# A late-weight schedule in a fused attention and mixture-of-experts kernel: logits in three parts, one more resident piece, buffers laid out by when they die

## The chip, the cores and the metric

The kernel runs on one core of one Trainium2 chip. The metric is device time in microseconds (us), the median of the runs shown. TensorE (PE) does matrix products and transposes, VectorE (DVE) and ScalarE (ACT) work on vectors and read the matrix results from PSUM, GpSimd (POOL) works on vectors in SBUF and issues DMAs, and SyncE (SP) issues DMAs.

## The reference

Attention with one extra zero logit in the denominator, and on its output a soft mixture of eight experts (32 slots, four per expert). Cut to what matters:

```python
# q, k, v: (8, 12, 448, 64)
scores = q @ k.T / sqrt(64);  m = scores.max(-1);  e = exp(scores - m)
attn_out = (e / (e.sum(-1) + exp(-m) + 1e-9)) @ v
x = attn_out as (3584, 768)                     # 12 heads side by side

logits = x @ phi                                # (3584, 32)
d = softmax of logits over the 3584 tokens      # one column per slot
slot_input = d.T @ x                            # (32, 768)
for e in range(8):                              # four slots per expert
    slot_out[e] = relu(slot_input[e] @ w1[e]) @ w2[e]    # 768 -> 1024 -> 768
c = softmax of logits over the 32 slots
out = c @ slot_out                              # (3584, 768)
```

The logits of a token need all twelve heads of its batch entry. The softmax over tokens needs all batch entries, so the experts can run only after the last attention tile.

## The kernel before

**Pairs and steps.** A unit u (0 to 23) is a pair of batch entries and a pair of heads; six units in a row make one group of two batch entries, and there are four such groups. Attention runs in steps n; unit u begins at step 7u. Step n computes one score tile (stage_S, line 200, whose row maximum DVE takes at line 208) and, ten steps behind (LAG), one transposed score tile (stage_ST: lines 236 and 241, with the exponential on ACT at line 245). The maximum reaches stage_ST as a mask md, which stage_MT (lines 214 to 226, on ACT and POOL) makes at step 7u+7. stage_AV (line 271) multiplies the exponentials by the values at steps 7u+13 to 7u+18; stage_AVout, stage_den and stage_N (lines 281 to 299) normalise, and stage_X (lines 345 and 347) transposes the result x to xt.

**An order written out by hand.** Nothing is reordered: a dictionary `plan` maps a step and a place in it ("small", then the step's stage_S, "value", stage_ST, "end", "load") to functions, and every engine and every DMA queue takes its instructions in that order. An engine does not keep step with the others: it runs ahead until an instruction has to wait, and everything behind that instruction waits too. POOL's instruction queue holds its vector work, the q and k loads and all weight loads (line 129). SP's holds the value loads (line 98).

**Values.** load_v fills `vr`, of which there is one; stage_V (line 250) casts it to bf16 into v65 or v66 and sets a column of ones (line 252). Both are planned at step 7u+9, the cast first and then the load for the next unit.

**Buffers.** All attention buffers are slices of one SBUF tile `block`, laid out by the dictionary `parts`. PSUM is a ring of three buffers (`slot`), handed out in program order, beside one for the value product (`av`).

**Mixture.** For each group of six units, mixture() plans, from step n = 42 bp + 62 on, the logits (line 379: 24 matmuls, four for each of the six head pairs, into one PSUM buffer, which ACT copies to lT at lines 386 and 387), the running maximum and exponential over tokens, slot_in (line 429, which reads the x of all six units) and the softmax over slots. In the last group five head pairs are summed at step n - 2 and the sixth at step n. There the experts follow: experts_hidden (line 553) with w1, and after the loop the product with w2 (line 642), the spread over partitions (line 651) and the output tiles (lines 665 to 670).

**Weights.** w1 and w2 come as 32 pieces of 768 KB: 16 of w1 first, then 16 of w2. The first WRES pieces have a place of their own in `wres` and are loaded during attention, one in nearly every unit. The others go into `rooms`, stretches of `block` over dead attention buffers:

```python
for n, i in ((end - 4, 0), (end + 3, 1), (end + 10, 2), (end + 12, 3), (end + 12, 4),
             (end + 12, 5), (end + 20, 6), (end + 27, 7), (end + 27, 8)):
    at(n, "load", lambda i=i: load_w(WRES + i))        # end = 168
```

The functions that the change touches:

Of the kernel before, what the change touches and what calls it, by code (L numbers as in the profile page):

```python
# [13 lines left out]
ALU = mybir.AluOpType  # L14
# [2 lines left out]
P = 64  # L17
LAG = 10
AV0 = (13, 14, 14, 15, 16, 17, 18)
WRES = 23  # L20


@with_exitstack
def kernel(
# [10 lines left out]
    nc = tc.nc  # L35

    B, H, S, D = q.shape
    DD = H * D
# [4 lines left out]
    TB = S // P  # L43
    KC = DD // 128
    FK = F // 128
    HP = H // 2
    BP = B // 2
    U = BP * HP
    C3 = TB // 2
    N2 = 2 * S  # L50
    G = E // 4
# [11 lines left out]

    HW = (KC // 2) * F
    parts, size = {}, 0
    for name, n, bufs in (("qr", N2, 1), ("kr", N2, 1), ("qk0", 2 * N2, 1), ("qk1", 2 * N2, 1),
                          ("vr", 2 * N2, 1), ("md0", N2, 1), ("v65", 2 * TB * 66, 1),
                          ("qk2", 2 * N2, 1), ("md1", N2, 1), ("v66", 2 * TB * 66, 1),
                          ("et", N2, 4), ("xu", 4 * TB * 65, 1),
                          ("x", N2, HP + 1), ("xt", N2, HP)):  # L70
        parts[name] = size, n, bufs
        size += n * bufs


    rooms = [i * HW for i in range(6)]
    rooms += [size - G * DD - HW, size - G * DD - 3 * HW, size - G * DD - 2 * HW]
    assert rooms[5] + HW <= parts["x"][0] + N2 <= rooms[7] and rooms[6] >= parts["xt"][0]
    block = const.tile([128, size], BF16, name="block")
    wres = const.tile([128, WRES, HW], BF16, name="wres")

    def buf(name, i):
        o, n, bufs = parts[name]
        return block[:, ds(o + (i % bufs) * n, n)]

    def room(i):

# [2 lines left out]
    def slot(shape, dtype=F32):  # L89
        return ring.tile(shape, dtype, tag="r", name="ps")  # L90
# [17 lines left out]
    def load_v(u):  # L108
        t_ = buf("vr", 0).bitcast(F32).rearrange("p (h n) -> p h n", h=2)
        RAW[u, "vr"] = load(u, t_, v, nc.sync if u else nc.gpsimd)  # L110
# [137 lines left out]
    def stage_V(u):  # L248
        t_ = buf(f"v6{5 + u % 2}", 0).rearrange("p (h t e) -> p h t e", h=2, e=66)
        nc.gpsimd.tensor_copy(t_[:, :, :, ds(0, D)],  # L250
                              RAW.pop((u, "vr")).rearrange("p h (t d) -> p h t d", t=TB))
        nc.gpsimd.memset(t_[:, :, :, ds(D, 1)], 1.0)
        V65[u] = t_
# [40 lines left out]
    def stage_N(u):  # L294
        xv = XU.pop(u)
        rec = small.tile([128, 2, TB], F32, tag="rec", name="rec", bufs=1)
        nc.vector.reciprocal(rec, DEN.pop(u))  # L297
        x = buf("x", u + 4).rearrange("p (s n) -> p s n", s=TB)
        nc.gpsimd.tensor_tensor(  # L299
            x.rearrange("p s (h d) -> p h s d", h=2), xv[:, :, :, ds(0, D)],  # L300
            rec.unsqueeze(3).broadcast_to([128, 2, TB, D]), op=ALU.mult)
        X[u] = x
# [12 lines left out]
    def stage_last(u):  # L315
        av = AV.pop(u)
        ems = DEN.pop(u)
        drec = small.tile([128, 2, TB], F32, tag="rec", name="rec", bufs=1).rearrange("p b g -> p (b g)")
        x = buf("x", u + 4).rearrange("p (s n) -> p s n", s=TB)
        main = av[:, :, ds(0, 2 * C3 * 65)].rearrange("p b (g e) -> p b g e", e=65)  # L320
        rest = av[:, :, ds(2 * C3 * 65, 65)]
        nc.vector.scalar_tensor_tensor(
# [35 lines left out]
    last_state = {}  # L358

    def mixture(bp, n, at):  # L360
# [9 lines left out]
        mx = small.tile([128, 8], F32, tag="mx", name="mx")  # L370
        sm = small.tile([128, 8], F32, tag="sm", name="sm")

        def logits_part(js):
            if js[0] == 0:
                last_state["lg"] = slot([128, 2, 128])
            ps = last_state["lg"]
            for j in js:
                for i, x in enumerate(groups(XT.pop(bp * HP + j))):
                    nc.tensor.matmul(ps[ds(32 * i, 32), ds(0, x.shape[1]), :], phi[:, j, :], x,
                                     start=(j == 0), stop=(j == KC - 1),  # L380
                                     tile_position=(0, 32 * i))

        def logits(js=range(KC)):
            logits_part(js)
            ps = last_state.pop("lg")
            nc.scalar.copy(lT[:, 0, :], ps[:, 0, :])
            nc.scalar.copy(lT[ds(0, 96), 1, :], ps[ds(0, 96), 1, :])

        def slot_max():
            if first:  # L390
# [80 lines left out]
            nc.scalar.copy(cT[ds(96, 32), bp, ds(0, 128)], ps[ds(96, 32), 0, :])  # L471

        if final:
            at(n - 2, "end", lambda: logits_part(range(KC - 1)))
            at(n, "end", lambda: logits((KC - 1,)))
            at(n + 2, "small", slot_max)
            at(n + 2, "end", gate_logits)
            at(n + 3, "small", slot_exp)
# [8 lines left out]
            at(n + 11, "small", gate_out)  # L487
            last_state["gate_T"] = gate_T
        else:
            at(n, "end", logits)  # L490
            at(n + 2, "end", slot_max)
            at(n + 3, "small", gate_logits)
            at(n + 5, "end", slot_exp)
# [67 lines left out]
    def at(n, where, f):  # L561
        plan.setdefault((n, where), []).append(f)

    for u in range(U):
        n = u * TB
# [2 lines left out]
        if u + 2 < U:  # L568
            at(n + 3, "load", lambda u=u: load_qk(u + 2))
        at(n + 7, "value", lambda u=u: stage_MT(u))  # L570
        at(n + 9, "load", lambda u=u: stage_V(u))
        if u + 1 < U:
            at(n + 9, "load", lambda u=u: load_v(u + 1))
        for m in sorted(set(AV0)):
            at(n + m, "value", lambda u=u, m=m: [
                stage_AV(u, [t for t in range(TB) if AV0[t] == m], part) for part in range(2)])
# [11 lines left out]
    for bp in range(BP):  # L588
        mixture(bp, (bp * HP + HP - 1) * TB + 27, at)

    for i, u in enumerate(sorted((*range(2, U - 1), 9, 16))):
        at(u * TB + 5, "load", lambda i=i: load_w(i))
    at(4, "load", late_constants)
    stage_T(0, "qr")
    stage_T(0, "kr")

    end = TB * U
    for n, i in ((end - 4, 0), (end + 3, 1), (end + 10, 2), (end + 12, 3), (end + 12, 4),
                 (end + 12, 5), (end + 20, 6), (end + 27, 7), (end + 27, 8)):
        at(n, "load", lambda i=i: load_w(WRES + i))  # L600
    last = max(n for n, _ in plan)

# [98 lines left out]
```

## Time and profile before

| | us |
|---|---|
| median of 3 runs | 343.98 |
| all runs | 346.65, 343.98, 342.94 |
| profiled execution, whole time | 345.78 |
| its span in the trace | 344.0 |

| engine | busy us | share of the span |
|---|---|---|
| PE | 289.1 | 84% |
| DVE | 255.8 | 74% |
| ACT | 207.5 | 60% |
| POOL | 202.8 | 59% |

The trace begins a little after the execution does and ends a little before it, so the span is shorter than the whole time. A row of a timeline gives start, duration, engine, line, operation, result and operands, count, and in brackets how long the engine had stood and what ended that. A row of the windows gives the busy time of each engine in a stretch (PE, weight loads, DVE, ACT, POOL, with instruction counts), the granted PE clock as a share of full speed, the busy share of the DMA engines and GB/s.

### The profile page before, as it was taken

The numbers are of one execution on the slowest core, as the hardware profiler recorded it, in microseconds if no ns is written. First come the engines' busy times: TensorE is split into PE (matmuls) and PEld (weight loads), VectorE is DVE, ScalarE is ACT, GpSimd is POOL, SyncE is SP. The second block draws the span as 40 slices with busy tenths as digits, with TensorE's granted clock in tenths as the row PEclk, the third lists the DMA queues.
The fourth block names the chain that finished last, engine by engine and source line by source line (L and its number), as shares of the span: only waits on it lengthen the run. The fifth ranks groups of instructions, "written<-read, shape, count | busy, mean of one in ns | idle before, by whom it ended". The sixth has DMA issues, their size and how long they took to land.

```text
span 344.0 us, 13196 instructions
## 1 busy us (share of the span) xinstructions
PE 289.1 (84%) x5864; PEld 161.7 (47%) x5864; DVE 255.8 (74%) x352; ACT 207.5 (60%) x327; POOL 202.8 (59%) x317
## 2 busy tenths in 40 slices
PE   2689999999999999987989979899989856858770
PEld 1335555555555565554655545465555433422110
DVE  2999898999889899988789979789877156016440
ACT  3037787777686677866677758676778840104340
POOL 8356676788767877767767866577636842200000
PEclk9999999999999999999999999999999985895555
DMA  6664799878898979988596999887864599945997
GB/s 87 115 99 93 138 195 168 166 160 156 169 196 143 210 147 197 194 155 160 106 193 129 215 200 150 149 155 147 163 147 84 108 182 216 214 84 207 396 399 281
DMA packets 30056, 59.09 MB, mean 172 GB/s; under 512 B 4048, under 2 KB 22224, under 8 KB 30000
## 3 DMA queue, kind: packets, MB, share of 16 engines
q0 software_dynamic: 19344, 36.69, 61.6%
q1 hardware_dynamic: 10656, 21.57, 19.0%
q8 instruction: 46, 0.75, 0.9%
q14 instruction: 10, 0.08, 0.1%
HBM read 83.46 MB, written 11.01 MB: 275 GB/s over the span
## 4 chain that ended last, share of the span: by engine, by line
PE 58%; ACT 14%; DMA 11%; DVE 8%; issue 5%; POOL 1%; SPq 0%; ACTq 0%; DVEq 0%; POOLq 0%
PE av L271 16%; PE ps L200 11%; PE ps L236 11%; PE ps L241 8%; ACT block L245 7%; PE ps L188 7%; DMA block<-in_moe_w_dram 6%; DVE m L208 5%; DMA out_dram<-wres 4%; ACT block L281 4%; ACT block L284 2%; PE ps L665 1%; DMA wres<-in_k_dram 1%; PE ps L429 1%; PE ps L212 1%
## 5 line engine op out<-in xcount | busy, mean ns | idle before, releaser
L208 DVE TENSOR_REDUCE m<-ps 128x2 bf16<-128x896 f32 x168 | 181.7, 1095 | 25.0 <-PE ps L200 21.9
L245 ACT ACTIVATE block<-ps 128x896 bf16<-128x896 f32 x168 | 154.0, 918 | 64.5 <-PE ps L241 58.5
L271 PE MATMUL av<-block 64*128 64x65 bf16 (+1 forms) x2688 | 82.8, 193 | 6.3 <-ACT block L284 2.3
L271 PEld LDWEIGHTS <-block 64*128 64x128 bf16 (+1 forms) x2688 | 70.0, 97 | 33.4 <-ACT block L284 9.5
L236 PE MATMUL ps<-block,ones 64*64 64x448 bf16 x672 | 69.1, 368 | 2.3 <-ACT block L245 0.9
L241 PE MATMUL ps<-block 64*64 64x448 bf16 x672 | 66.2, 352 | 1.9 <-issue 1.9
L220 POOL TENSOR_TENSOR block<-mt,nmask 128x768 bf16<-128x768 bf16 x24 | 35.2, 1466 | 45.9 <-ACT mt L214 43.6
L200 PE MATMUL ps<-block 64*128 64x448 bf16 x288 | 54.0, 372 | 3.3 <-DVE m L208 0.9
L200 PEld LDWEIGHTS <-block 64*128 64x128 bf16 x288 | 18.2, 94 | 55.2 <-issue 54.6
L299 POOL TENSOR_TENSOR block<-block,rec 128x896 bf16<-128x896 f32 x23 | 38.7, 1681 | 1.5 <-DVE rec L297 1.5
L98 POOL DMA_DIRECT2D block<-in_q_dram x46 | 29.4, 643 | 7.1 <-PE ps L188 6.8
L191 DVE COPY block<-ps 128x896 bf16<-128x896 bf16 x48 | 27.8, 616 | 4.4 <-PE ps L188 4.4
L236 PEld LDWEIGHTS <-ones 64*64 64x64 bf16 x672 | 25.6, 105 | 10.0 <-issue 2.9
L98 POOL DMA_DIRECT2D block<-in_k_dram x46 | 27.9, 626 | 2.3 <-issue 2.3
L188 PE MATMUL ps<-ident,block 128*64 128x128 bf16 x644 | 26.3, 229 | 3.2 <-issue 2.3
L188 PEld LDWEIGHTS <-block 128*64 128x64 bf16 x644 | 21.8, 114 | 5.7 <-issue 4.7
L241 PEld LDWEIGHTS <-block 64*64 64x64 bf16 x672 | 23.6, 107 | 0.4 <-issue 0.3
L665 PE MATMUL ps<-wres,cT 32*128 32x384 bf16 x56 | 19.1, 500 | 4.9 <-DVE wres L668 3.5
L250 POOL CAST block<-block 128x896 bf16<-128x896 f32 x24 | 22.3, 927 | 1.0 <-DMA block<-in_v_dram 1.0
L668 DVE COPY wres<-ps 128x768 f32<-128x768 f32 x14 | 13.4, 958 | 11.7 <-PE ps L665 8.4
L347 DVE COPY block<-ps 128x896 bf16<-128x896 bf16 x24 | 14.8, 616 | 9.6 <-PE ps L345 9.6
L668 ACT COPY wres<-ps 128x768 f32<-128x768 f32 x14 | 11.1, 799 | 14.7 <-DMA out_dram<-wres 9.8
(112 smaller groups left out, 241.3 us busy)
## 6 DMA issues: line engine op xcount, KB each, us to landing
wres<-in_moe_w_dram POOLq DMA_DIRECT2D x23, 768.0 KB, 9.0
out_dram<-wres SPq DMA_DIRECT2D x28, 384.0 KB, 4.7
block<-in_v_dram SPq DMA_DIRECT2D x46, 224.0 KB, 5.1
block<-in_moe_w_dram POOLq DMA_DIRECT2D x9, 768.0 KB, 13.6
block<-in_q_dram POOLq DMA_DIRECT2D x46, 112.0 KB, 4.4
block<-in_k_dram POOLq DMA_DIRECT2D x46, 112.0 KB, 5.4
block<-in_v_dram POOLq DMA_DIRECT2D x2, 224.0 KB, 4.4
wres<-in_q_dram POOLq DMA_DIRECT2D x2, 112.0 KB, 3.3
```

Of the source, the lines that this page charges most:

```text
L98: eng.dma_start(out=t_[ds(b * P, P), :, :], in_=src[bp * 2 + b, ds(hp * 2, 2)].rearrange("h (p t) d -> p h (t d)", t=TB))
L188: nc.tensor.transpose(ps[ds(h * D, D), :, ds(t * P, P)], r[:, h, ds(t * D, D)], ident)
L191: nc.vector.tensor_copy(t_, ps)
L200: nc.tensor.matmul(ps[:, h, ds(0, S)], QT[u][hs, b, ds(c * 128, 128)], KT[u][hs, b, :], start=True, stop=True)
L208: nc.vector.tensor_reduce(m[:, :, s], ps[:, :, ds(0, S)], axis=AX.X, op=ALU.max)
L220: nc.gpsimd.tensor_tensor(md[:, :, ds(0, C3 * 128)].rearrange("p b (c n) -> p b c n", c=C3), mt.unsqueeze(1).unsqueeze(1).broadcast_to([12 ...
L236: nc.tensor.matmul(ps[ds(b * P, P), h, ds(0, S)], ones[hs, :], MD[u][hs, b, :], start=True, stop=False)
L241: nc.tensor.matmul(ps[ds(b * P, P), h, ds(0, S)], KT[u][hs, b, ds(t * P, P)], QT[u][hs, b, :], start=False, stop=True)
L245: nc.scalar.activation(et, ps[:, :, ds(0, S)], AF.Exp, scale=scale)
L271: nc.tensor.matmul(o, et[bs, h, ds(c * 128, w)], V65[u][bs, h, t, ds(0, 65)], start=(t == 0 and h == 0 and c == 0), stop=(t == TB - 1), sk ...
L299: nc.gpsimd.tensor_tensor(x.rearrange("p s (h d) -> p h s d", h=2), xv[:, :, :, ds(0, D)], rec.unsqueeze(3).broadcast_to([128, 2, TB, D]), ...
L668: (nc.vector.tensor_copy if i % 2 else nc.scalar.copy)(o.rearrange("p (g n) -> p g n", g=2), ps[:, :, ds(0, 384)])
```

## The change

- **Logits in parts.** The six head pairs are summed as three pairs of two, at steps n - 28, n - 14 and n, each into a PSUM buffer of its own. The first part is copied to lT by ACT; the others are copied by ACT into lc and added to lT by POOL. In the last group the third part is summed as one head pair at n - 2 and one at n, and DVE adds it to lT from PSUM.
- **xt** then needs two buffers instead of six.
- **A 24th resident piece**, loaded in unit 13 beside that unit's own; eight late pieces instead of nine.
- **The layout of `block`** follows the order in which buffers die; one of the seven x buffers (x0) stands apart from the other six, beside qr and kr. Room 0 lies over qr, kr and x0; room 1 over qk0 and vr; room 2 over vr, qk1 and md0; room 3 over v65 and xu; rooms 4 and 5 over qk2, md1, v66 and et; rooms 6 and 7 over the x buffers.
- **Steps of the late pieces:** 163, 167, 171, 176, 180, 180, 195 and 195.
- **Value casts** of units 22 and 23 are planned at steps 7u+6 and 7u+5 instead of 7u+9, and the load for unit 23 goes with the cast of unit 22.

```diff
--- before.py
+++ after.py
@@ -17,7 +17,7 @@
 P = 64
 LAG = 10
 AV0 = (13, 14, 14, 15, 16, 17, 18)
-WRES = 23
+WRES = 24
 
 
 @with_exitstack
@@ -63,24 +63,35 @@
 
     HW = (KC // 2) * F
     parts, size = {}, 0
-    for name, n, bufs in (("qr", N2, 1), ("kr", N2, 1), ("qk0", 2 * N2, 1), ("qk1", 2 * N2, 1),
-                          ("vr", 2 * N2, 1), ("md0", N2, 1), ("v65", 2 * TB * 66, 1),
-                          ("qk2", 2 * N2, 1), ("md1", N2, 1), ("v66", 2 * TB * 66, 1),
-                          ("et", N2, 4), ("xu", 4 * TB * 65, 1),
-                          ("x", N2, HP + 1), ("xt", N2, HP)):
+
+    def part(name, n, bufs=1):
+        nonlocal size
         parts[name] = size, n, bufs
         size += n * bufs
 
-
-    rooms = [i * HW for i in range(6)]
-    rooms += [size - G * DD - HW, size - G * DD - 3 * HW, size - G * DD - 2 * HW]
-    assert rooms[5] + HW <= parts["x"][0] + N2 <= rooms[7] and rooms[6] >= parts["xt"][0]
+    for name, n in (("pad0", HW - 3 * N2), ("qr", N2), ("kr", N2), ("x0", N2),
+                    ("qk0", 2 * N2), ("vr", 2 * N2), ("qk1", 2 * N2), ("md0", N2),
+                    ("v65", 2 * TB * 66), ("xu", 4 * TB * 65), ("pad1", 200),
+                    ("qk2", 2 * N2), ("md1", N2), ("v66", 2 * TB * 66)):
+        part(name, n)
+    part("et", N2, 4)
+    part("x", N2, HP)
+    part("xt", N2, 2)
+
+
+    rooms = [i * HW for i in range(8)]
+    assert parts["x"][0] <= rooms[6] + HW and rooms[7] + HW <= size - G * DD
+    assert parts["xu"][0] + 4 * TB * 65 + 200 >= rooms[4] and parts["xt"][0] <= size - G * DD
     block = const.tile([128, size], BF16, name="block")
     wres = const.tile([128, WRES, HW], BF16, name="wres")
 
     def buf(name, i):
         o, n, bufs = parts[name]
         return block[:, ds(o + (i % bufs) * n, n)]
+
+    def xbuf(u):
+        i = (u + 4) % (HP + 1)
+        return buf("x", i - 1) if i else buf("x0", 0)
 
     def room(i):
 
@@ -295,7 +306,7 @@
         xv = XU.pop(u)
         rec = small.tile([128, 2, TB], F32, tag="rec", name="rec", bufs=1)
         nc.vector.reciprocal(rec, DEN.pop(u))
-        x = buf("x", u + 4).rearrange("p (s n) -> p s n", s=TB)
+        x = xbuf(u).rearrange("p (s n) -> p s n", s=TB)
         nc.gpsimd.tensor_tensor(
             x.rearrange("p s (h d) -> p h s d", h=2), xv[:, :, :, ds(0, D)],
             rec.unsqueeze(3).broadcast_to([128, 2, TB, D]), op=ALU.mult)
@@ -316,7 +327,7 @@
         av = AV.pop(u)
         ems = DEN.pop(u)
         drec = small.tile([128, 2, TB], F32, tag="rec", name="rec", bufs=1).rearrange("p b g -> p (b g)")
-        x = buf("x", u + 4).rearrange("p (s n) -> p s n", s=TB)
+        x = xbuf(u).rearrange("p (s n) -> p s n", s=TB)
         main = av[:, :, ds(0, 2 * C3 * 65)].rearrange("p b (g e) -> p b g e", e=65)
         rest = av[:, :, ds(2 * C3 * 65, 65)]
         nc.vector.scalar_tensor_tensor(
@@ -370,21 +381,28 @@
         mx = small.tile([128, 8], F32, tag="mx", name="mx")
         sm = small.tile([128, 8], F32, tag="sm", name="sm")
 
-        def logits_part(js):
-            if js[0] == 0:
-                last_state["lg"] = slot([128, 2, 128])
-            ps = last_state["lg"]
+        def logits(js, close=True):
+            if "lg" not in last_state:
+                last_state["lg"] = slot([128, 2, 128]), js[0]
+            ps, j0 = last_state["lg"]
             for j in js:
                 for i, x in enumerate(groups(XT.pop(bp * HP + j))):
                     nc.tensor.matmul(ps[ds(32 * i, 32), ds(0, x.shape[1]), :], phi[:, j, :], x,
-                                     start=(j == 0), stop=(j == KC - 1),
+                                     start=(j == j0), stop=(close and j == js[-1]),
                                      tile_position=(0, 32 * i))
-
-        def logits(js=range(KC)):
-            logits_part(js)
-            ps = last_state.pop("lg")
-            nc.scalar.copy(lT[:, 0, :], ps[:, 0, :])
-            nc.scalar.copy(lT[ds(0, 96), 1, :], ps[ds(0, 96), 1, :])
+            if not close:
+                return
+            del last_state["lg"]
+            for r, rows in ((0, 128), (1, 96)):
+                a, o = lT[ds(0, rows), r, :], ps[ds(0, rows), r, :]
+                if j0 == 0:
+                    nc.scalar.copy(a, o)
+                elif final and js[-1] == KC - 1:
+                    nc.vector.tensor_tensor(a, a, o, op=ALU.add)
+                else:
+                    b = lc.rearrange("p (r i) n -> p r (i n)", r=2)[ds(0, rows), r, :]
+                    nc.scalar.copy(b, o)
+                    nc.gpsimd.tensor_tensor(a, a, b, op=ALU.add)
 
         def slot_max():
             if first:
@@ -471,8 +489,10 @@
             nc.scalar.copy(cT[ds(96, 32), bp, ds(0, 128)], ps[ds(96, 32), 0, :])
 
         if final:
-            at(n - 2, "end", lambda: logits_part(range(KC - 1)))
-            at(n, "end", lambda: logits((KC - 1,)))
+            at(n - 28, "end", lambda: logits((0, 1)))
+            at(n - 14, "end", lambda: logits((2, 3)))
+            at(n - 2, "end", lambda: logits((4,), close=False))
+            at(n, "end", lambda: logits((5,)))
             at(n + 2, "small", slot_max)
             at(n + 2, "end", gate_logits)
             at(n + 3, "small", slot_exp)
@@ -487,7 +507,8 @@
             at(n + 11, "small", gate_out)
             last_state["gate_T"] = gate_T
         else:
-            at(n, "end", logits)
+            for j in range(0, HP, 2):
+                at(n - 7 * (HP - 2 - j), "end", lambda j=j: logits((j, j + 1)))
             at(n + 2, "end", slot_max)
             at(n + 3, "small", gate_logits)
             at(n + 5, "end", slot_exp)
@@ -568,9 +589,10 @@
         if u + 2 < U:
             at(n + 3, "load", lambda u=u: load_qk(u + 2))
         at(n + 7, "value", lambda u=u: stage_MT(u))
-        at(n + 9, "load", lambda u=u: stage_V(u))
+        cast = n + {U - 2: 6, U - 1: 5}.get(u, 9)
+        at(cast, "load", lambda u=u: stage_V(u))
         if u + 1 < U:
-            at(n + 9, "load", lambda u=u: load_v(u + 1))
+            at(cast, "load", lambda u=u: load_v(u + 1))
         for m in sorted(set(AV0)):
             at(n + m, "value", lambda u=u, m=m: [
                 stage_AV(u, [t for t in range(TB) if AV0[t] == m], part) for part in range(2)])
@@ -588,15 +610,15 @@
     for bp in range(BP):
         mixture(bp, (bp * HP + HP - 1) * TB + 27, at)
 
-    for i, u in enumerate(sorted((*range(2, U - 1), 9, 16))):
+    for i, u in enumerate(sorted((*range(2, U - 1), 9, 13, 16))):
         at(u * TB + 5, "load", lambda i=i: load_w(i))
     at(4, "load", late_constants)
     stage_T(0, "qr")
     stage_T(0, "kr")
 
     end = TB * U
-    for n, i in ((end - 4, 0), (end + 3, 1), (end + 10, 2), (end + 12, 3), (end + 12, 4),
-                 (end + 12, 5), (end + 20, 6), (end + 27, 7), (end + 27, 8)):
+    for n, i in ((end - 5, 0), (end - 1, 1), (end + 3, 2), (end + 8, 3), (end + 12, 4),
+                 (end + 12, 5), (end + 27, 6), (end + 27, 7)):
         at(n, "load", lambda i=i: load_w(WRES + i))
     last = max(n for n, _ in plan)
 
```

## The prediction

> **What bounds the kernel now.** I read the page first (busy shares and chain), then the windows by stage, then PE's timeline of the tail, then the timelines of POOL and PE around the moved value casts.
>
> ```profile
> span 344.0 us, 13196 instructions
> PE 289.1 (84%) x5864; PEld 161.7 (47%) x5864; DVE 255.8 (74%) x352; ACT 207.5 (60%) x327; POOL 202.8 (59%) x317
> PE 58%; ACT 14%; DMA 11%; DVE 8%; issue 5%; POOL 1%; SPq 0%; ACTq 0%; DVEq 0%; POOLq 0%
> 250.00:275.00 25.00, 21.99 (x514) 12.00 (x513) 13.94 (x18) 21.14 (x32) 14.07 (x25) 1.00 0.55 115
> 285.00:295.00 10.00, 7.38 (x91) 3.26 (x89) 4.36 (x13) 0.42 (x1) 2.29 (x4) 0.53 1.04 215
> 295.00:305.00 10.00, 7.21 (x143) 3.81 (x136) 0.36 (x2) 1.08 (x2) 1.80 (x1) 1.00 0.96 199
> 315.00:325.00 10.00, 7.79 (x26) 1.94 (x23) 5.75 (x6) 4.43 (x7) 0.00 (x0) 0.50 1.02 395
> ...
> block<-in_moe_w_dram POOLq DMA_DIRECT2D x9, 768.0 KB, 13.6
> ```
>
> Attention (to about 278 us) is set by PE, with DVE and ACT close behind. Then comes a serial stretch, and from 285 us the DMA engines are full (1.04, 0.96 of their time) while they were half idle (0.55) just before: the late weight pieces all come at once. From 313 us the output transfers fill them again (1.02, 395 GB/s), so the last 30 us only shift with their start. What the late pieces cost stands in PE's timeline:
>
> ```profile
> 288.86 8.05 PE L553 MATMUL ps<-wres,block 128*32 128x512 bf16 x96 [0.42 <-DVE block L541]
> ...
> 298.87 1.64 PE L642 MATMUL ps<-wres 128*32 128x384 bf16 x35 [0.37 <-DVE wres L634]
> ...
> 301.33 2.06 PE L642 MATMUL ps<-block,wres 128*32 128x384 bf16 x36
> 306.72 1.55 PE L642 MATMUL ps<-block,wres 128*32 128x384 bf16 x29 [3.33 <-DMA block<-in_moe_w_dram]
> ...
> 309.31 0.80 PE L651 MATMUL ps<-wres,spread 128*128 128x384 bf16 x2 [0.72 <-DVE wres L647]
> 286.03 1.07 POOL L129 DMA_DIRECT2D block<-in_moe_w_dram  x2 [3.78 <-PE ps L429]
> ```
>
> PE runs L642 for 4.5 us, stands 3.33 us for the last piece, and needs 1.55 us more. So all that earlier weights can give is 3.33 us; the rest of L642 (6.1 us) stays. The last two pieces are issued at 286.03, behind L429 (slot_in, which frees the x buffers).
>
> **The change part by part.** Times are of the profiled execution: span 344.0, whole time 345.78, which is 1.8 above the median 343.98. I sum differences and take them off the median.
>
> *24th resident piece, six of eight late pieces earlier: -3.3.* One piece fewer falls into the full stretch, and pieces 0 to 3 are now freed at steps 163, 167, 171 and 176 (a step is one score tile; pair u begins at step 7u) instead of 164, 171, 178 and 180. At the quoted 199 to 215 GB/s a piece of 768 KB (0.79 MB) takes 3.7 to 3.9 us. Pieces 0 to 2 then fit into the half-idle time before 277; 3, 4 and 5 follow, and the last two, issued after L429 at about 288, land near 297 to 299. L642 needs them only after three quarters of its 6.1 us, about 305. The stall goes: -3.33, with some 6 us to spare.
>
> *Value casts of the last two pairs at step u+6 and u+5: +1.9.* This is what I expect to be late next. The value tile vr has one buffer, so the load of pair 22 starts when the cast of pair 21 ends, and that cast hasn't moved:
>
> ```profile
> 249.15 0.93 POOL L250 CAST block<-block 128x896 bf16<-128x896 f32 x1
> ...
> 250.07 0.62 POOL L129 DMA_DIRECT2D wres<-in_moe_w_dram  x1
> 254.32 0.21 POOL L290 TENSOR_TENSOR den<-block,em 128x14 f32<-128x14 f32 x1 [3.62 <-ACT block L284]
> 254.62 0.25 POOL L291 TENSOR_SCALAR den<-den 128x14 f32<-128x14 f32 x1
> 257.14 1.47 POOL L220 TENSOR_TENSOR block<-mt,nmask 128x768 bf16<-128x768 bf16 x1 [2.26 <-ACT mt L214]
> 258.56 0.40 POOL L226 TENSOR_TENSOR block<-mt,nmask 128x128 bf16<-128x128 bf16 x1
> 258.92 1.68 POOL L299 TENSOR_TENSOR block<-block,rec 128x896 bf16<-128x896 f32 x1
> 260.55 0.93 POOL L250 CAST block<-block 128x896 bf16<-128x896 f32 x1
> ...
> 261.47 0.61 POOL L129 DMA_DIRECT2D block<-in_moe_w_dram  x1
> ```
>
> ```profile
> L98 SPq DMA_DIRECT2D block<-in_v_dram x4: 595/602/607, 250.1 to 262.1; - x4
> DMA to landing us min/median/max: 7.9/8.0/8.2
> ```
>
> ```profile
> 259.38 0.37 PE L200 MATMUL ps<-block 64*128 64x448 bf16 x2
> ...
> 259.87 0.38 PE L236 MATMUL ps<-block,ones 64*64 64x448 bf16 x2
> ...
> 260.47 0.36 PE L200 MATMUL ps<-block 64*128 64x448 bf16 x2
> ```
>
> SP issues the two halves at 250.10 and 250.70; beside the weight piece of 250.07 they take 8.0 us, so the second lands at 258.7. Before, the cast came after pair 22's mask (257.14) and normalisation (258.92) and found the data there. Now it stands ahead of both in POOL's order, behind only the sums of 254.62. POOL waits to 258.75; the cast and its memset take 0.92 (249.15 to 250.07), the mask 1.82 (257.14 to 258.96). The instruction lists of the two built kernels also show that L226 and the memset L252 now wait for POOL's own instruction before them, 48 times in all. Such a wait costs 0.14: L291 starts 0.09 after L290's end, where L226 starts 0.05 before L220's. Two of them fall here. The mask is ready at 258.75 + 0.92 + 1.82 + 0.28 = 261.8, but L236 of step 164 wants it at 259.87: PE stands 1.9 us. Behind it on PE lie the scores of steps 165 to 167, paced 1.09 apart (259.38, 260.47) and feeding DVE, and no later stage has room to make it up. Behind it on POOL are the normalisation and late piece 0 (at 263.5 instead of 261.47), with time in hand. The load of pair 23 begins 2 us earlier, ahead of piece 0, and its cast waits for nothing. Bounds: 0 (data by 255.7, at the 5.0 us that is the median of all value loads) to +2.3 (both halves at the longest, 8.2, and a cast and mask each 0.1 longer). I take 1.9, since both pairs in this window show 7.9 to 8.2.
>
> The other 46 own waits cost POOL about 6.4 us in all, in its time before L220, where it waits for mt (2.26 here): 0 on the path, up to 1 if some pair has no such room.
>
> *Logits in three parts: +0.1 in the stream, +0.25 and +0.15 at the end.* The 24 matmuls become three groups of 8, in steps of the same kind:
>
> ```profile
> 85.41:86.76 1.35, 1.23 (x33) 1.00 1.18 280
> 95.76:97.88 2.12, 2.00 (x56) 1.00 1.20 243
> ```
>
> ```profile
> 97.11 0.84 PE L379 MATMUL ps<-block,phi 128*32 128x256 bf16 x24
> ```
>
> ```profile
> 98.06 0.26 ACT L386 COPY ld<-ps 128x128 f32<-128x128 f32 x1
> 98.20 0.27 ACT L387 COPY ld<-ps 96x128 f32<-96x128 f32 x1
> ```
>
> ```profile
> L449 POOL TENSOR_TENSOR lc<-lc,mx 128x256 f32<-128x256 f32 x4 | 2.4, 611 | 7.6 <-DVE stat L408 5.3 <-DVE mx L448 2.3
> L334 DVE TENSOR_TENSOR block<-av,rec 128x128 bf16<-128x128 f32 x1 | 0.3, 282 | 0.0
> ```
>
> The step with the logits is 0.77 us longer than its twin, less than the matmuls' own 0.84. Three groups of 0.28 make the same sum; the PSUM ring turns one place further in eight more steps, so that the next score waits for the DVE maximum instead of an exponential. By the twin step that maximum ends near 87.0, where the small group ends too: 0 to 0.3 each, and I take 0.1 for all. Seven more pairs of ACT copies (0.4 each) and seven pairs of POOL additions (half of 611 ns and a start, about 0.4 each) lie in ACT's idle 40% and POOL's waits. Not at step 174: there the copies stand ahead of the last exponentials, whose gaps hide half: +0.25 (0 to 0.4; the additions also delay the last POOL normalisation, up to 0.3). Part three ends in two DVE additions (282 ns by L334) in place of two ACT copies with a handover: +0.15 (-0.1 to +0.3).
>
> *24th piece in the stream: +0.3.* It is a transfer of 3.7 us in pair 13, beside loads that have a pair's time to land. What such traffic costs is seen in PE's waits for nothing that the profile shows, between 25 and 275 us:
>
> ```profile
> PE ps L188 <- issue: 2.3, 3, 1.2
> ...
> PE ps L241 <- issue: 1.9, 1, 1.9
> PE av L271 <- issue: 1.8, 2, 1.2
> ```
>
> Six us over some 22 pieces make 0.3 for one more; from -1.5 to +1.5, since such waits can move with every shift of a transfer.
>
> *Clock after L642: -0.4.*
>
> ```profile
> 307.00:308.00 1.00, 1.00 (x29) 0.58 (x17) 0.00 (x0) 0.00 (x0) 0.00 (x0) 0.99 0.00 0
> 308.00:309.00 1.00, 0.59 (x7) 0.24 (x3) 0.70 (x1) 0.37 (x1) 0.00 (x0) 0.50 0.00 0
> ```
>
> The granted clock falls to half at 308, right after the stall. Without the stall PE is busy from L553 to the end of L642, and L651 (0.80 at half) should run at full clock: -0.4 (-0.8 to 0).
>
> Sum: -3.33 + 1.9 + 0.1 + 0.25 + 0.15 + 0.3 - 0.4 = -1.0. The profiled time would be 344.8, the median 343.0.
>
> **The rivals.**
> A. *The value data land in time.* Then the cast costs nothing and the gain is 2.9: 341.1. For it: most loads take 5.0. Against: the weight piece is still issued right behind that cast.
> B. *The clock falls in the new wait.* A PE idle for 1.9 us out of a few may drop to half clock, as it did after 3.33 us of standing at 303.4; two steps paced 1.09 at full clock would then take some 0.8 longer each: +1.7, 344.7. Against: the 1.9 us wait of L241 above lies in a stretch whose clock stayed 1.00. The Trainium skill ("TensorE: Matmul & The Clock Gate", What's actually happening) says that a free-running window of about 3.4 us without activity halves the clock; by that rule 1.9 us of idling are too short, though it speaks against putting any wait here.
> C. *Slower: the ring of three PSUM buffers decides.* If each part, however short, costs its step the whole 0.77 (a wait for the buffer, not the matmuls), twelve parts in place of four add 8 x 0.77 = 6.2: 343.0 - 0.1 + 6.2 = 349.1. It decides where the DVE maximum ends later than the group. Against: the 0.77 is below the matmuls' 0.84.
> D. *The pieces are still late.* If the last two again need the 20 us that they took from 286.6 to 306.7, they land at 308.8, PE stalls as before, and all other terms stay: +2.1 + 0.4 = 2.5, 346.5. Against: fewer pieces are ahead of them.
>
> **How the numbers follow.** Forecast 0.52 (its own range 341.6 to 344.4), A 0.20, B 0.12, C 0.08, D 0.06; 0.02 for other shifts of the issue waits. About 1% is what a measurement of this kernel can tell from no change: below 340.5 and above 347.4. Below lie a third of A and a little of the forecast and the unnamed: 0.11. Above lie most of C, a quarter of D, a little of B and the unnamed: 0.12. The range reaches down to A with an issue wait less, up past B to D: 340.2 to 346.8.
>
> **What would show it.** Right: in PE's timeline no DMA wait inside L642; on POOL a wait of the second-last L250 for the value data of about 4 us, and L236 of step 164 some 1.9 us late; L651 in 0.4; no longer steps at the small logits groups than 0.3. Wrong: a value landing of 5 us (A), a clock below 1.00 near 262 (B), waits of L200 for DVE in the steps after logits (C), a DMA wait left at L642 (D).

## The result and the profile after

Over 20 runs each, the changed kernel takes 341.84 us (339.9 to 345.69) and the kernel before 344.63 us (342.42 to 349.15): ratio 0.9925, 95% interval 0.9899 to 0.9952. Faster, by 1.7 to 3.5 us, and within 1%. Two later series on other chips gave 0.9994 (0.9958 to 1.0029) and 0.9961 (0.9921 to 1.0001), both with intervals that reach 1. So the gain lies between nothing and some 0.8%, with 0.4% as the mean of the three, and the first figure is not to be taken alone. The profiled execution took 344.81 us (before 345.78). Executions over 1.5% above the fastest of their kernel are left out of the ratios below, four of six in e1_cast_back; its profile and those of a_third and e6_old_steps show such executions, and of them only lengths of stages are used.

The page of the changed kernel, its head and the issues of the late pieces:

```profile
span 343.0 us, 13224 instructions
PE 287.7 (84%) x5864; PEld 161.1 (47%) x5864; DVE 256.5 (75%) x354; ACT 209.7 (61%) x341; POOL 213.4 (62%) x331
...
PE 56%; ACT 15%; DMA 10%; DVE 9%; issue 4%; POOL 2%; SPq 1%; ACTq 0%; DVEq 0%; POOLq 0%
...
block<-in_moe_w_dram POOLq DMA_DIRECT2D x8, 768.0 KB, 8.9
```

PE's timeline of the tail, and two windows (PE busy, weight loads, DVE, ACT, POOL, clock, DMA share, GB/s):

```profile
293.85 6.78 PE L574 MATMUL ps<-wres,block 128*32 128x512 bf16 x96 [0.42 <-DVE block L562]
...
302.59 2.78 PE L664 MATMUL ps<-wres 128*32 128x384 bf16 x64 [0.37 <-DVE wres L656]
305.20 2.77 PE L664 MATMUL ps<-block,wres 128*32 128x384 bf16 x64
...
309.04 0.48 PE L673 MATMUL ps<-wres,spread 128*128 128x384 bf16 x2 [0.84 <-DVE wres L669]
```

```profile
295.00:305.00 10.00, 8.82 (x156) 4.30 (x152) 1.15 (x5) 1.50 (x3) 2.46 (x3) 0.91 0.75 156
315.00:325.00 10.00, 7.49 (x23) 1.82 (x21) 4.59 (x6) 3.99 (x5) 0.00 (x0) 0.50 1.02 395
```

L574 is the old L553, and L664 the old L642. L664 runs through without a wait: 5.38 us from 302.59, where it took 9.40 with the stall. The DMA engines are no longer full before it ends (0.75), and L673 (the old L651) runs at full clock, 0.48 for 0.80. The output phase is as full as before (1.02). But L664 starts 3.7 us later than it did (302.59 after 298.87). Of this, 2.05 us come before step 158 (it begins at 252.52 after 250.47), and 2.95 between that and the last value product. L574 gives 1.27 back, 6.78 us for 8.05, as the granted clock returned to full sooner behind its start. The first line is of the kernel before, the second of the changed one:

```profile
294.00:295.00 1.00, 1.00 (x20) 0.42 (x16) 0.00 (x0) 0.00 (x0) 0.00 (x0) 0.83 1.16 240
296.00:297.00 1.00, 1.00 (x16) 0.37 (x12) 0.35 (x2) 0.00 (x0) 0.44 (x1) 0.62 1.13 238
```

Full clock is back at about 294.3, 5.5 us into L553, and at about 296.8, 2.9 us into L574. The change doesn't make this gain: in the other two profiles of the changed kernel L574 takes 8.07 and 7.52 us, and 6.66 to 8.07 in all that follow. For most of the 2.95 us the timelines of POOL and PE show the cause:

```profile
251.20 0.93 POOL L261 CAST block<-block 128x896 bf16<-128x896 f32 x1
252.19 0.16 POOL L263 MEMSET block<- 128x14 bf16 x1
252.25 0.62 POOL L140 DMA_DIRECT2D wres<-in_moe_w_dram  x1
...
257.58 0.25 POOL L302 TENSOR_SCALAR den<-den 128x14 f32<-128x14 f32 x1
261.24 0.93 POOL L261 CAST block<-block 128x896 bf16<-128x896 f32 x1 [3.41 <-DMA block<-in_v_dram]
262.23 0.16 POOL L263 MEMSET block<- 128x14 bf16 x1
262.31 1.47 POOL L231 TENSOR_TENSOR block<-mt,nmask 128x768 bf16<-128x768 bf16 x1
263.85 0.40 POOL L237 TENSOR_TENSOR block<-mt,nmask 128x128 bf16<-128x128 bf16 x1
```

```profile
262.86 0.54 PE L282 MATMUL av<-block 64*128 64x65 bf16 x16
264.30 0.38 PE L247 MATMUL ps<-block,ones 64*64 64x448 bf16 x4 [0.90 <-POOL block L237]
```

The cast of unit 22 stands 3.41 us for its data, the mask behind it ends at 264.2, and PE waits 0.90 us for it at step 164. That wait is the prediction's, at half its size, because PE came to it late: it had stood 1.33 us, until 254.4, for nothing that the profile shows.

**How to compare single profiles here.** The stream up to step 158 is nearly the same work in every kernel, and yet step 158 begins anywhere from 246.1 to 255.6 us in the profiles below. Two of the changed kernel alone begin it at 252.5 and 247.9, with 5.5 and 2.7 us of PE waits up to there for nothing that the profile shows, and in the first the clock is at half from about 150.0 to 153.4. So spans of single profiles can't be compared to a microsecond; lengths of stages can. Two are used: from the start of step 158 to the end of the last value product ("end of attention"), and the length of the w2 product (L642).

| kernel | ratio to before (95%) | end of attention, us | w2 product, us |
|---|---|---|---|
| before | | 27.14 | 9.40 |
| changed | 0.9925 (0.9899 to 0.9952) | 30.09 | 5.38 |
| a_again, the same | 0.9994 (0.9958 to 1.0029) | 30.26 | 5.39 |
| a_third, the same | 0.9961 (0.9921 to 1.0001) | 30.33 | 5.38 |
| e3_logits_alone | 1.0012 (0.9984 to 1.0040) | 28.19 | 9.88 |
| e10_casts_alone | 1.0035 (1.0001 to 1.0069) | 29.94 | 8.43 |
| e1_cast_back | 0.9840 (0.9774 to 0.9905) | 28.33 | 5.38 |
| e1_again, the same | 0.9878 (0.9839 to 0.9918) | 28.02 | 5.38 |
| e2_piece_behind | 0.9954 (0.9915 to 0.9993) | 33.61 | 5.38 |
| e5_nine_late | 0.9963 (0.9933 to 0.9994) | 30.10 | 5.39 |
| e6_old_steps | 0.9980 (0.9946 to 1.0014) | 30.42 | 5.38 |
| e7_back_nine | 0.9930 (0.9887 to 0.9973) | 28.86 | 7.47 |
| e8_layout_alone | 0.9966 (0.9925 to 1.0007) | 27.29 | 6.80 |
| e9_whole_even | 0.9898 (0.9873 to 0.9922) | 26.52 | 7.39 |

### The profile page after: what moved, and what is told of

Same layout as the page of the kernel before. It is cut to its first block, busy times and chain, and to the rows that moved or that the text cites. A ratio compares the mean times of both kernels' runs of the same rounds, so it can differ in the third digit from the quotient of the medians.

```text
span 343.0 us, 13224 instructions
## 1 busy us (share of the span) xinstructions
PE 287.7 (84%) x5864; PEld 161.1 (47%) x5864; DVE 256.5 (75%) x354; ACT 209.7 (61%) x341; POOL 213.4 (62%) x331
## 4 chain that ended last, share of the span: by engine, by line
PE 56%; ACT 15%; DMA 10%; DVE 9%; issue 4%; POOL 2%; SPq 1%; ACTq 0%; DVEq 0%; POOLq 0%
PE av L282 15%; PE ps L247 10%; PE ps L211 10%; ACT block L256 7%; PE ps L252 7%; PE ps L199 7%; DMA out_dram<-wres 4%; ACT block L292 4%; DVE m L219 4%; DMA block<-in_v_dram 2%; DMA block<-in_k_dram 2%; PE ps L574 2%; PE ps L664 2%; ACT block L295 2%; DVE wres L690 1%
## 5 line engine op out<-in xcount | busy, mean ns | idle before, releaser
L282 PE MATMUL av<-block 64*128 64x65 bf16 (+1 forms) x2688 | 83.9, 193 | 9.2 <-issue 4.9
L252 PE MATMUL ps<-block 64*64 64x448 bf16 x672 | 65.5, 354 | 0.0
L231 POOL TENSOR_TENSOR block<-mt,nmask 128x768 bf16<-128x768 bf16 x24 | 35.2, 1465 | 26.2 <-ACT mt L225 23.8
L247 PEld LDWEIGHTS <-ones 64*64 64x64 bf16 x672 | 25.7, 105 | 10.2 <-issue 2.9
L687 PE MATMUL ps<-wres,cT 32*128 32x384 bf16 x56 | 17.8, 455 | 5.8 <-DVE wres L690 2.5
```

The lines of the kernel that those rows point to most:

```text
L231: nc.gpsimd.tensor_tensor(md[:, :, ds(0, C3 * 128)].rearrange("p b (c n) -> p b c n", c=C3), mt.unsqueeze(1).unsqueeze(1).broadcast_to([12 ...
L247: nc.tensor.matmul(ps[ds(b * P, P), h, ds(0, S)], ones[hs, :], MD[u][hs, b, :], start=True, stop=False)
L252: nc.tensor.matmul(ps[ds(b * P, P), h, ds(0, S)], KT[u][hs, b, ds(t * P, P)], QT[u][hs, b, :], start=False, stop=True)
L282: nc.tensor.matmul(o, et[bs, h, ds(c * 128, w)], V65[u][bs, h, t, ds(0, 65)], start=(t == 0 and h == 0 and c == 0), stop=(t == TB - 1), sk ...
```

## The experiments

**The moved casts.** e1 undoes them in the changed kernel; late piece 1, whose room lies over vr, then has to go three steps later, behind the cast. e10 does them alone in the kernel before.

```diff
# e1_cast_back, e1_again, against the changed kernel
-        cast = n + {U - 2: 6, U - 1: 5}.get(u, 9)
+        cast = n + 9
-    for n, i in ((end - 5, 0), (end - 1, 1), (end + 3, 2), ...
+    for n, i in ((end - 5, 0), (end + 2, 1), (end + 3, 2), ...
# e10_casts_alone, against the kernel before
-        at(n + 9, "load", lambda u=u: stage_V(u))           # load_v(u + 1) likewise
+        cast = n + {U - 2: 6, U - 1: 5}.get(u, 9)
+        at(cast, "load", lambda u=u: stage_V(u))
```

e1_cast_back: 

> The changed kernel with the last two value casts back at step u+9; late pieces 1 and 2 go to steps 170 and 171, behind the cast that frees vr. Theory 1 (the moved casts cost, because POOL stands for the value data): the 3.41 us wait of POOL and the 0.9 us wait of PE for the mask at step 164 are gone, and the time falls by 0.5 to 1.5 us against the changed kernel, ratio to before near 0.989; no DMA wait comes back at the w2 product, since the pieces still land before three quarters of it are done. Rival (the moved casts are what lets the pieces in early): pieces 1 and 2 slip by 3 to 5 us, a DMA wait of 1 us or more returns at the w2 product, and the ratio goes to 0.995 or above.

e1_again: 

> The changed kernel with the last two value casts back at u+9, a second time, on the chip of the two others. Theory: 28.2 to 28.5 us from step 158 to the last value product, no DMA wait at the w2 product, 1 to 2.5 us faster than before (ratio 0.988 to 0.996). Rival: no faster than the changed kernel, ratio 0.996 or above.

e10_casts_alone: 

> The kernel before with the last two value casts at steps u+6 and u+5, and nothing else. Theory (POOL stands for the value data of unit 22, and the mask behind it is late): POOL waits 3 to 5 us before that cast, PE 1 to 2.2 us for the mask at step 164; from step 158 to the last value product 28.5 to 29.5 us instead of 27.1; time 1 to 2 us above before, ratio 1.003 to 1.006. Rival (the cost comes from the new layout or the parts, not from the casts): 27.1 us and a ratio of 0.998 to 1.002.

With the casts back, the end of attention is 28.33 and 28.02 us instead of 30.09 to 30.33: 2.0 us less. No DMA wait came back. In the second profile the mask is made before the cast, and PE has no wait at step 164:

```profile
254.90 1.47 POOL L231 TENSOR_TENSOR block<-mt,nmask 128x768 bf16<-128x768 bf16 x1 [2.59 <-ACT mt L225]
256.44 0.40 POOL L237 TENSOR_TENSOR block<-mt,nmask 128x128 bf16<-128x128 bf16 x1
256.80 1.69 POOL L310 TENSOR_TENSOR block<-block,rec 128x896 bf16<-128x896 f32 x1
258.43 0.93 POOL L261 CAST block<-block 128x896 bf16<-128x896 f32 x1
```

The ratio of e1_cast_back rests on two runs, so the second series is the one to read: 0.9878. In e10 the casts alone make the old kernel's end of attention 2.8 us longer, and its time 0.35% (0.01 to 0.69%) longer, since part is given back at the w2 product, where the last piece is awaited less. On POOL and PE of e10:

```profile
255.63 0.93 POOL L250 CAST block<-block 128x896 bf16<-128x896 f32 x1 [4.73 <-PE ps L241]
```

```profile
258.45 0.38 PE L236 MATMUL ps<-block,ones 64*64 64x448 bf16 x4 [2.32 <-POOL block L226]
```

PE's L241 had long ended when that cast began; the wait is for the value data. Their second half landed at 255.5, and the changed kernel's profile names them for the same wait (3.41, in_v_dram). The rival (layout or parts as the cause of this wait) falls.

**Why the value data are late.** e2 issues the last resident piece behind the cast of unit 22.

```diff
-        at(u * TB + 5, "load", lambda i=i: load_w(i))
+        at(u * TB + (6 if u == U - 2 else 5), "load", lambda i=i: load_w(i))
```

> The changed kernel with the last resident weight piece issued behind the cast of unit 22 instead of in front of it. Theory 1 (the value load is slow because a weight piece is issued in the same microsecond): the load of unit 22 lands in 4 to 5.5 us instead of 8.6, POOL waits under 1 us, PE has no wait for the mask at step 164, and the time falls by 0.5 to 1.5 us against the changed kernel (ratio near 0.989). Rival (the value load is late by itself, since it starts only after the cast before it): the wait of POOL stays above 2.5 us and the time is that of the changed kernel, 0.9925.

Half of it came true: the two halves of the value load of unit 22 landed after 3.4 and 4.6 us, its cast stood 1.20 us, and step 164 had no wait. But the load of unit 23 now had the weight piece beside it and late piece 0 right behind:

```profile
253.55 0.93 POOL L261 CAST block<-block 128x896 bf16<-128x896 f32 x1 [1.20 <-PE ps L390]
...
254.59 0.63 POOL L140 DMA_DIRECT2D wres<-in_moe_w_dram  x1
...
258.80 0.59 POOL L140 DMA_DIRECT2D block<-in_moe_w_dram  x1
265.86 0.93 POOL L261 CAST block<-block 128x896 bf16<-128x896 f32 x1 [6.47 <-PE ps L252]
```

```profile
DMA to landing us min/median/max: 3.4/6.6/10.6
```

That cast stood 6.47 us, as the halves of its load took 8.6 and 10.6. PE stood 3.99 us for the mask of unit 23, and the clock then fell to half, from about 268.9 to 279.1; the end of attention grew to 33.6 us by both together.

```profile
269.00:270.00 1.00, 0.00 (x0) 0.00 (x0) 0.00 (x0) 0.00 (x0) 0.92 (x2) 0.50 0.65 98
```

The theory's mechanism holds and its forecast of time fails (0.9954 for 0.989): the wait went one unit on.

**The logits in parts.** e3 puts mixture()'s new parts into the kernel before, its layout untouched.

```diff
-            at(n, "end", logits)
+            for j in range(0, HP, 2):
+                at(n - 7 * (HP - 2 - j), "end", lambda j=j: logits((j, j + 1)))
# and in the last group the parts at n - 28, n - 14, n - 2 and n
```

> The kernel before with the logits in three parts, and nothing else of the change. Theory 1 (groups of 8 cost their matmuls and little more): steps with a small group are 0.3 to 0.35 us longer than their twins, the three shortened ones 0.45 shorter, the end 0.4 to 0.6 later: +0.5 to +1.7 us, ratio 1.0015 to 1.005. Rival ring (each extra group costs a PSUM place): over +4 us, ratio above 1.012. Rival gain (the parts take work off the end): below 0.998.

Ratio 1.0012 (0.9984 to 1.0040): no gain, and none of the ring's 4 us. The end of attention is 1.05 us longer (28.19). In the windows of the changed kernel a step with a small group stands against its twin:

```profile
86.33:87.67 1.34, 1.23 (x32) 0.55 (x28) 1.34 (x2) 1.22 (x3) 1.34 (x4) 1.00 1.03 168
97.36:99.03 1.67, 1.56 (x42) 0.68 (x37) 1.52 (x2) 1.43 (x4) 0.47 (x2) 1.00 1.07 204
```

0.33 us more for 8 matmuls; in the kernel before 0.77 more for 24. By this one pair of steps, three small groups cost 0.2 us more than one large one.

**One piece fewer, or earlier?** e5 has nine late pieces at the changed kernel's steps, e6 eight at the old ones.

```diff
# e5_nine_late
-    for i, u in enumerate(sorted((*range(2, U - 1), 9, 13, 16))):
+    for i, u in enumerate(sorted((*range(2, U - 1), 9, 16))):
+    at(end + 12, "load", lambda: load_w(WRES - 1))
# e6_old_steps
-    for n, i in ((end - 5, 0), (end - 1, 1), (end + 3, 2), (end + 8, 3), (end + 12, 4),
+    for n, i in ((end - 4, 0), (end + 3, 1), (end + 10, 2), (end + 12, 3), (end + 12, 4),
```

e5_nine_late: 

> The changed kernel with nine late pieces again: the 24th resident piece is not loaded during attention but at step 180, into its own place, between late pieces 5 and 6. Theory 1 (the earlier issue of the others fills the half-idle stretch, and that alone nearly suffices): the DMA engines are full until about 306 instead of 302, the wait at the w2 product is 0 to 1 us, the stream is 0 to 1 us faster without the second piece of unit 13; the time stays within 1 us of the changed kernel (ratio 0.990 to 0.995). Rival (one piece fewer is what takes the stall away): a DMA wait of 2 us or more at the w2 product, ratio 0.998 or above.

e6_old_steps: 

> The changed kernel with the first six late pieces planned at the steps of before (164, 171, 178, 180, 180, 180) instead of 163, 167, 171, 176, 180, 180; still eight late pieces. Theory (either of the two, one piece fewer or an earlier issue, suffices, since nine early pieces showed no DMA wait): DMA wait at the w2 product of 0 to 0.5 us, time within 1 us of the changed kernel. Rival (both are needed): a DMA wait of 1.5 us or more.

Neither has a DMA wait: the w2 product takes 5.39 and 5.38 us. e5's:

```profile
298.94 2.78 PE L665 MATMUL ps<-wres 128*32 128x384 bf16 x64 [0.37 <-DVE wres L657]
301.55 2.77 PE L665 MATMUL ps<-block,wres 128*32 128x384 bf16 x64
```

Either of the two takes the stall away, but both kernels also start the w2 product later, since both keep the moved casts. The ratio of e5, 0.9963, lies above its 0.990 to 0.995, as that of the changed kernel does in its later series. e7 has nine pieces and takes the casts back as well:

> The changed kernel with the last two value casts back at step u+9 (pieces 1 and 2 at steps 170 and 171) and nine late pieces, the 24th loaded at step 180 into its own place. Theory: no wait of PE for the mask at step 164, no second piece in unit 13; from step 158 to the last value product 28.2 us instead of 30.1; a DMA wait of 0 to 1 us at the w2 product; 1 to 2.5 us faster than the changed kernel, ratio to before 0.985 to 0.990. Rival (casts back and nine pieces together run out of time): DMA wait of 2 us or more and a ratio above 0.993.

```profile
300.96 1.46 PE L665 MATMUL ps<-block,wres 128*32 128x384 bf16 x29 [1.77 <-DMA block<-in_moe_w_dram]
```

Now 1.77 us of the wait are back. Attention is 1.2 to 1.5 us shorter than with the moved casts (28.86), and nine pieces are then too many. The wait misses its 0 to 1 us and the time (0.993) its 0.985 to 0.990.

**The layout without the parts.** e8 is the kernel before with the buffers by when they die: whole logits, six xt buffers, casts at u+9, nine late pieces. e9 also keeps the value load of unit 23 clear of late piece 0.

```diff
# e8_layout_alone, against the kernel before: the new order of parts, x0 and xbuf, and
+    rooms = [i * HW for i in (0, 1, 2, 3, 4, 5, 8, 6, 7)]
+    for n, i in ((end - 5, 0), (end + 2, 1), (end + 5, 2), (end + 10, 3), (end + 12, 4),
+                 (end + 12, 5), (end + 20, 6), (end + 27, 7), (end + 27, 8)):
# e9_whole_even, against e8
-        cast = n + 9
+        cast = n + {U - 1: 8}.get(u, 9)
-    for n, i in ((end - 5, 0), (end + 2, 1), ...
+    for n, i in ((end - 1, 0), (end + 1, 1), ...
```

e8_layout_alone: 

> The kernel before with the layout by death alone: whole logits in one group with six xt buffers, 23 resident pieces, casts at u+9; nine late pieces at steps 163, 170, 173, 178, 180, 180, 188 (over xt), 195 and 195. The two filler stretches are left out for want of space. Theory: nothing of the cost of the logits in parts (from step 158 to the last value product 27.1 us as before, and the stream as before); the w2 product waits 0 to 1 us for a DMA; 3 to 4.5 us faster than before, ratio 0.987 to 0.991. Rival (the parts are needed for the gain): a DMA wait of 2 us or more, ratio 0.995 or above.

e9_whole_even: 

> The layout alone (whole logits, 23 resident pieces, nine late ones), with the value load of unit 23 given the DMA engines to itself: late piece 0 is planned at step 167 behind the sums of POOL, the cast of unit 23 at step 169 behind the last normalisation but one, piece 1 right behind it. Theory (a value load beside a weight piece takes 8 us, alone 3.3 to 5): the load of unit 23 lands in 3.3 to 5.5 us, its cast waits for nothing, piece 1 leaves 1 to 1.5 us earlier after the mask of unit 23 than in the layout alone, and the DMA wait at the w2 product falls from 1.1 to 0 to 0.5 us; ratio to before 0.985 to 0.993. Rival (the engines are full anyway, so the last piece lands when it did): the DMA wait stays at 1 us or above.

The waits at the w2 product of e8 and e9, and the value load of unit 23 in e9:

```profile
302.49 1.46 PE L653 MATMUL ps<-block,wres 128*32 128x384 bf16 x29 [1.10 <-DMA block<-in_moe_w_dram]
```

```profile
301.18 1.46 PE L653 MATMUL ps<-block,wres 128*32 128x384 bf16 x29 [1.69 <-DMA block<-in_moe_w_dram]
```

```profile
DMA to landing us min/median/max: 3.1/3.4/3.6
```

e8 keeps the old end of attention (27.29) and 1.10 us of the wait, a little over the forecast; its ratio, 0.9966, misses the 0.987 to 0.991. In e9 the value load takes 3.4 us, as the theory said, but the DMA wait is 1.69, not under 0.5, which is what the rival had forecast. Yet the rival's reason (the last piece lands when it did) doesn't hold: the wait for it ended 52.5 us after the start of step 158, in e8 53.9. The w2 product began 46.6 us after step 158 where e8 took 48.5, so PE came earlier still; 0.9 of these 1.9 us are the w1 product (7.04 us for 7.95). The time is good all the same, 0.9898.

**The changed kernel again.**

a_again: 

> The changed kernel once more, unaltered, for a second profile and for times on the same chip as the three that follow. All theories: ratio to before 0.990 to 0.995; no DMA wait at the w2 product, which takes 5.4 us; POOL stands 3 to 5 us for the value data before the cast of unit 22, and PE 0.9 to 2.2 us for the mask at step 164, by where PE happens to be.

a_third: 

> The changed kernel a third time, since its first two ratios to before, 0.9925 and 0.9994, lie apart. Theory (the new wait at step 164 costs 2 to 3 us when it also halves the clock, and 1 us when it doesn't, while the w2 product always gains 4): ratio 0.992 to 0.998; in the trace a mask wait of PE of 0.9 to 2.3 us, with a stretch of half clock of 3.4 us behind it where the wait is 2 us or longer. Rival (the spread is that of the chips alone): ratio outside 0.990 to 0.9995.

PE and the clock around step 164 in a_again:

```profile
259.44 0.38 PE L247 MATMUL ps<-block,ones 64*64 64x448 bf16 x4 [2.21 <-POOL block L237]
```

```profile
257.52:260.93 3.41, 1.49 (x34) 0.67 (x33) 1.07 (x2) 0.84 (x2) 3.33 (x4) 0.99 0.45 135
260.00:261.00 1.00, 1.00 (x29) 0.48 (x26) 0.65 (x1) 0.88 (x1) 1.00 (x2) 0.93 0.45 167
261.00:262.00 1.00, 1.00 (x11) 0.57 (x8) 0.76 (x2) 0.81 (x2) 0.99 (x3) 0.50 0.00 0
264.00:265.00 1.00, 1.00 (x37) 0.55 (x33) 1.00 (x2) 0.49 (x2) 0.46 (x1) 0.86 1.05 215
```

The wait is 2.21 us, and the clock is then at half from about 260.9 to 264.3. a_third shows the same after a wait of 1.75 us, e5, e6 and e10 after 2.0, 2.2 and 2.3; the first profile of the changed kernel, with 0.90, doesn't. So a_third's boundary of 2 us was set too high. The ratio of a_again, 0.9994, misses its 0.990 to 0.995; a_third's 0.9961 is as forecast. Why the three series differ is not shown: the lengths in the table hardly do, and one profile with a short L574 (the first) does not stand for its series.

## Why the prediction was right, step by step

The time was right (341.84 for 343.0, range 340.2 to 346.8) and so was the shape: a large gain at the w2 product, most of it given back in front of it. The total was right in part by luck. The gains were larger than forecast, -4.0 and -0.7 for -3.3 and -0.4, and the end of attention cost more: 2.95 to 3.2 us (30.09 to 30.33 after 27.14) for some 2.2 (1.9, 0.25 and a share of 0.1). Together these make about -1.6, where the forecast was -1.0 and the ratios of the three series make -0.2 to -2.6. By its terms:

- **Late pieces, -3.3: the mechanism right, the size -4.0.** 9.40 became 5.38 in every profile of the changed kernel. I had counted the 3.33 us wait alone; the matmuls around the break were slower too (128 in 6.07 us with the wait taken off, 5.38 in one run; why is not shown, the clock was at 0.99 to 1.00). The room to spare was smaller than the 6 us forecast: the last piece was issued at 291.75 and took 11.8 us, so it landed at 303.5, and three quarters of L664 were done at about 306.6. That leaves 3 us.
- **Two causes for one gain.** I took the missing piece and the earlier issue together. e5 and e6 show that either is enough while the casts are moved; with the casts back, e7 shows that nine pieces are too many.
- **Moved casts, +1.9: the mechanism and the total right (2.0, e1 against the changed kernel), the split in part wrong.** I had the mask 11.3 us behind the start of step 158 (261.8 after 250.47). The masked product of step 164 starts 11.8, 11.6 and 11.6 us behind it in the three profiles, 9.1 in e1_again. The wait was 0.90, 2.21 and 1.75 us, by how late PE itself came. In the two longer ones the clock then halved, which I had made a rival (B, 0.12) instead of a part of this term. It cost little here and not B's 1.7 us: the end of attention is 30.26 and 30.33 us with it, 30.09 without. By its start at step 167, unit 23's last score was 15.3 us behind step 158 in a_again and 12.4 in e1_again, 2.9 us apart; 0.7 of that is made up by the end of attention, where I had seen no room for it.
- **The rule I weighed there.** The Trainium skill ("TensorE: Matmul & The Clock Gate", What's actually happening) has a free-running window of about 3.4 us decide. The trace agrees with the length: the half clock in a_again lasts from 260.9 to 264.3. I read from it that 1.9 us of idling are too short, and the trace doesn't agree with that: the window from 257.52 to 260.93 had PE busy for 1.49 of 3.41 us, and the clock fell at its end. Low activity was enough here; PE's longest idle stretch there was 2.21 us, so a wholly idle window wasn't needed.
- **Own waits of POOL, 0.14 each.** L263 now starts 0.99 after its cast, 0.87 before, and L237 1.54 after L231, 1.42 before: 0.12 each. e8 and e9, whose layout leaves out the two fillers, have the old 0.87 and 1.42; that the fillers are the cause is not shown, since their buffers of xt differ too.
- **Logits, +0.1 in the stream and +0.25 at the end: too small.** Each extra small group added 0.33 to its step, 0.05 over its matmuls, so the ring (C) is out. In e3 the end of attention grew by 1.05 us, of which 0.33 are the group at step 160. The other 0.7 may be the copies and additions at step 174, but are not shown to be: before and e3 have a PE wait of 0.57 and 0.41 us in this stage for nothing that the profile shows. A cleaner pair is e1_again and e8, with 28.02 and 27.29 and such waits of 0.68 and 0.59: 0.33 of their difference is there at step 167, and 0.4 comes behind it. They also differ in one late piece and the fillers. The DVE additions (+0.15) cost nothing that can be seen: from the last value product to L553's first matmul it is 11.25 us before and 11.24 after.
- **24th piece, +0.3: not seen.** Waits for nothing that the profile shows ranged from 2.7 to 7.1 us in the changed kernel and were 3.9 in e5, which lacks the piece in the stream. Their spread is over ten times the term.
- **Clock after L642, -0.4: right, and larger.** L651 to the first output matmul took 1.53 us for 1.85, and the output phase 32.4 for 32.8: -0.7.

A (data in time) and D (pieces still late) didn't happen, though the first series' 341.84 lies nearer to A's 341.1 than to the forecast. D's price was also added up wrongly: PE standing until 308.8 instead of 306.7 makes +2.1, and the further 0.4 is not derived.

**What beats both.** Taking the moved casts back (e1, 0.9878) or leaving the logits whole with the new layout (e9, 0.9898) beat the kernel before on one chip, 340.32 and 340.89 us against 344.12. Against the changed kernel e1's advantage is shown in the trace (2.0 us at the end of attention); their times come from different series.

## What to carry to other kernels

A stage planned earlier on an in-order queue is only as early as its data: find the load behind it, what that load shares the DMA engines with, and what stands behind the waiting instruction. An early cast that frees a buffer for one transfer can hold up a mask that the busiest engine needs. When the gain hangs on one wait, see whether several parts of a change each remove it, and keep the cheapest; and where single profiles differ by more than the effect, compare lengths of stages rather than spans.

## What the runs showed of the hardware

- A wait of PE of only 1.75 to 2.3 us in a busy stretch was followed by about 3.4 us at half clock in five profiles (a_again, a_third, e5, e6, e10), and one of 3.99 us by 10.2 us at half clock (e2); one of 0.90 us was not.
- The two 224 KB DMAs of a value load each landed 3.1 to 3.6 us after their issue when the next weight piece was issued 2.5 us behind them (unit 23 in e9), 7.9 to 8.2 beside one 768 KB weight piece (units 22 and 23 before), and up to 10.6 with a second one behind it (unit 23 in e2).
- With the buffers laid out anew in one SBUF tile, two POOL instructions of each unit started 0.12 us later behind POOL's own instruction before them; in e8 and e9, laid out without the fillers, they did not.
